# RWKV-6 attention and a tanh-shrink MLP on one core: empty TensorE instructions moved to the head of boot, and the first two weight loads put behind TensorE's work

## The chip, the cores and the metric

One Trainium2 chip, one NeuronCore of it. The time is device microseconds of one execution, from three runs of the kernel before: 545.66, 544.77 and 544.2, median 544.77 us. TensorE is called PE here (PEld is its weight load), VectorE DVE, ScalarE ACT, GpSimd POOL, SyncE SP. SP issues most of the DMAs.

## What is computed

```python
# r, k, v, w: (4, 8, 768, 48), u: (8, 48), f32
for t in range(S):
    cur = einsum('bhd,bhe->bhde', u * k_t, v_t)
    y_t = einsum('bhd,bhde->bhe', r_t, state + cur)
    state = w_t[..., None] * state + einsum('bhd,bhe->bhde', k_t, v_t)
x = y.transpose(0, 2, 1, 3).reshape(3072, 384)
h = x @ w_in            # 384 x 2048, weights of 64-bit width
g = h - tanh(h)
out = g @ w_out         # 2048 x 384
```

## The kernel before

The sequence of each batch is cut into two blocks of 384 tokens, eight blocks in all (`blocks`, line 1100). For one block the attention is computed in chunks of 64 tokens, for four pairs of heads, of which two at a time make a half (`HALVES`, `h1` the pairs 2 and 3, `h2` the pairs 0 and 1). The result `xT` (384 x 384, transposed) then runs through the MLP: for each of 16 tiles `f` of the hidden dimension, `first` (line 869) makes `h` with three products, `slight` (line 882) makes `g` from it on ACT and DVE, and `add` (lines 947 and 1001) multiplies `g` with `w_out`. The attention of the next block is spread among these tiles by a plan (line 1053) that says what runs at which `f`.

The order of all work on PE, SP, DVE and ACT is written out by hand: each engine runs its instructions in the order in which the Python code records them. An f32 product that is written once appears in the trace as two loads and two matmuls, so 24 written products of a group show as x48.

**Boot** (`boot`, line 1128) does the attention of block 0 before anything else. SP issues the inputs' loads and then the first raw weights. DVE scans the decays of half `h1` (`behind`, `before`), PE runs warm-up products on the identity (`passed`, `busy`; 94 of 16 columns, 11 of 512), and then, for `h1`: `own` (the products of k and r within a chunk), `turn_1` (six transposes), `earlier` (the products of k and r across the two decays), `update_half` (k by v), and later `from_scores` and `from_states`, which make the half's result in PSUM. In between and after come the same for `h2`. The masked copies of `own` and `earlier` into the scores are DVE's (line 502), `states_half` is a DVE scan (line 631), and `result_out` copies results into `late` and `xT` on ACT and DVE (line 729). In PE's order the second half runs `update_half(h2)`, `own(h2)`, one filler product, `earlier(h2)`, `from_states(h2)`, `from_scores(h2)`, and then the first tile of block 0 begins with `first` (line 871). The filler writes a PSUM tile of the first half's result, so it waits for ACT's copies of that result.

**The raw weights** come as 16 units of 768 KB (`load_weights`, line 248, in the order `UNITS`), each holding two tiles of `w_in` or `w_out` in 64-bit numbers. Five buffers hold them (`RAWS`). `convert` (line 253) makes f32 of one unit: three pieces on ACT (line 264) and one combination on DVE (line 268). `more_weights` issues the next unit's load on SP; `begin_behind(ins, then)` makes `then` wait for `ins`. Units 0 and 1 are `w_in` for the tiles 0 to 3, unit 2 is `w_out` for the tiles 0 and 1. The third load of boot waits for `own(h2)`, the fourth for `earlier(h2)`. In block 0 the pieces of conversion that ACT runs at tile `f` are counted in `PIECES`; ACT and DVE run in order, so a piece that moves changes what stands behind it.

**Empty instructions** on PE (`nop`, hint "apart") follow the products: `SPACED[i]` gives how many come after each product of `first` in block `i`, in the early and in the late tiles, and `add` puts one behind each of its own in most of block 0. PE's instructions are brought in by a DMA queue of their own, which the profile names "instruction".

The lines that the change touches are 76 and 80 (constants), `turn_1` (line 513) and `boot`.

Of the kernel before, what the change touches and what calls it, by code (L numbers as in the profile page):

```python
# [51 lines left out]
P = 128  # L52
# [20 lines left out]
RAWS = 5  # L73
LAG = 2
LAST = 5
PIECES = 0, 0, 2, 3, 3, 2, 4, 4, 3, 3, 3, 4, 4
UNITS = [(0, 0), (0, 1)] + [u for j in range(NF // 2 - 2) for u in ((1, j), (0, j + 2))] + [(1, NF // 2 - 2),
                                                                                      (1, NF // 2 - 1)]
LATE = 3
SPACED = (3, 0), (0, 3), (3, 2), (2, 3), (3, 2), (2, 3), (3, 0), (0, 0)  # L80

# [43 lines left out]
def kernel(  # L127
# [12 lines left out]
    nc = tc.nc  # L140
# [25 lines left out]
    ident = const.tile([P, P], F32, name="ident", tag="ident")  # L166
# [81 lines left out]
    def load_weights(n, queue):  # L248
        raw = conv.tile([P, 2 * DM, 2], I32, name="raw", tag="raw")
        src = weights[UNITS[n]].bitcast(I32).rearrange("p (n two) -> p n two", two=2)  # L250
        return *UNITS[n], raw, queue.dma_start(out=raw, in_=src)
# [46 lines left out]
    def scratch(ps):  # L298
        return ps.tile([P, 2, BANK], F32, name="att", tag="att")
# [14 lines left out]
    def begin_behind(ins, then):  # L314
        tc.add_manual_dep(then.ins, ins.ins.name, mybir.DependencyInfo(
            mybir.DependencyClass.Sync, mybir.DependencyReason.DATA))
# [3 lines left out]
    class Block:  # L320
# [186 lines left out]
        def own(self, ps, p0, **fill):  # L507
            return self.masked(ps, "k", "r", masks["diagonal"], p0, **fill)

        def earlier(self, ps, p0, **fill):  # L510
            return self.masked(ps, "post", "pre", masks["above"], p0, **fill)

        def turn_1(self, ps, p0):
            tp = scratch(ps)
            for p in range(UP):
                for c in range(NCP):
                    nc.tensor.transpose(tp[:, p, c * P:(c + 1) * P],
                                        self.chunk("post", p0 + p, 2 * c, n=2), ident)
            self.turned_as = tp

        def turn_2(self, p0):
# [347 lines left out]
    def first(xT, f, hp, apart=0):  # L869
        for kc in reversed(range(KC)):  # L870
            nc.tensor.matmul(hp, lhsT=w_in_sb[:, f, kc, :], rhs=xT[kc],  # L871
                             start=(kc == KC - 1), stop=(kc == 0))
            for _ in range(apart):
                nc.tensor.nop(nofuse=True, hint="apart")
        h = dense.tile([P, NB], F32, name="h", tag="h")
        return h, nc.scalar.activation(out=h, in_=hp, func=AF.Copy, scale=1.0 / UPSCALE)  # L876
# [228 lines left out]
    def more_weights(queue):  # L1105
        raws.append(load_weights(more_weights.n, queue))
        more_weights.n += 1
        return raws[-1][-1]
# [3 lines left out]
    def run(ops):  # L1112
        for op in ops:
            op()
# [13 lines left out]
    def boot(ps, pair, blk, later):  # L1128
        h1, h2 = HALVES
        blk.tiles["w"] = states0  # L1130
        for name, p0, n in (("w", h1 + 1, 1), ("w", h1, 1), ("k", h1, UP), ("r", h1, UP), ("w", h2, UP)):
            blk.load(name, p0, n)
        blk.load_v()
        blk.load("k", h2, UP)
        blk.load("r", h2, UP)
        more_weights(nc.sync)

        both = (h1, h1 + 1), (h2, h2 + 1)
        blk.behind(h1 + 1, 1)
        blk.behind(h1, 1)  # L1140
        blk.take_whole(h1, UP)
        blk.totals_by_column(h1)
        nc.scalar.copy(out=later_ident, in_=ident)
        blk.before(h1, UP)
        blk.times_behind(h1, UP)
        blk.times_u(h1, UP)
        own = blk.own(ps, h1, spare=94, ahead=5, late=6)
        blk.turn_1(ps, h1)
        blk.times_before(h1, UP)
        earlier = blk.earlier(ps, h1)  # L1150
        blk.behind(h2, UP)
        blk.take_whole(h2, UP)
        first_a, first_b = convert(*raws.pop(0), tiles=2)
        own()
        blk.turn_2(h1)
        blk.totals_by_column(h2)
        blk.update_half(pair, h1)
        begin_behind(blk.done, more_weights(nc.sync))
        blk.times_behind(h2, UP)
        blk.times_u(h2, UP)  # L1160
        blk.turn_1(ps, h2)
        blk.turn_2(h2)
        earlier()
        blk.results(ps)
        blk.result("from_scores", both[0])
        run(blk.states_half(h1))
        blk.result("from_states", both[0], True, apart=True)
        blk.before(h2, UP)
        blk.update_half(pair, h2)
        blk.times_before(h2, UP)  # L1170
        own = blk.own(ps, h2)
        own_scored = blk.done
        run(first_a[:1])
        blk.result_out((3,), [nc.scalar.copy] * 2)
        blk.result_out((2,))
        earlier = blk.earlier(ps, h2, ahead=1)
        scored = blk.done
        onwards = blk.states_half(h2)
        own()
        run(first_a[1:])  # L1180
        needed = 2 * KC - 2
        blk.fill_holes([nc.sync, nc.gpsimd], range(needed, 2 * KC))
        begin_behind(own_scored, more_weights(nc.sync))
        blk.fill_holes([nc.sync, nc.gpsimd], range(needed))
        begin_behind(scored, more_weights(nc.sync))
        later.load("w")
        second_a, second_b = convert(*raws.pop(0))
        third_a, third_b = convert(*raws.pop(0))
        run(second_a)
        more_weights(nc.sync)  # L1190
        blk.results(ps)
        blk.yp.reverse()
        blk.result("from_states", both[1], apart=True)
        earlier(1, 1)
        earlier(0, 1)
        for p in reversed(both[1]):
            blk.result("from_scores", (p,), True, more=True)
        later.load("k")
        more_weights(nc.sync)
        run(onwards)  # L1200
        run(first_b[:1])
        for p in reversed(both[1]):
            blk.result_out((p,), [nc.scalar.copy, nc.vector.tensor_copy])
        run(first_b[1:])
        run(third_a[:2])
        run(second_b)
        blk.held(0, NPAIR)
        return [(third_a[2], third_b)]
# [38 lines left out]
    for i, blk in enumerate(blocks):  # L1247
# [9 lines left out]
        for f in range(NF):  # L1257
# [4 lines left out]
            to = [acc[0], acc[1], hp, spare_a, spare_b, spare_a][now] if now < 6 else hp  # L1262
            h, made = first(here, f, to[:, 0:NB], SPACED[i][f > 12 + (i < 2)])
            if not i:
                made_up = converting(pieces, (PIECES[f] if f < len(PIECES) else 1) - 1)
                for op in ahead_of_h:
                    op()
                made_up += converting(pieces, 1 if f < len(PIECES) and PIECES[f] else 0)
            g, ahead_of_h, square, later_ops = slight(h, now, i, f)
# [184 lines left out]
```

## Time and profile before

| | |
|---|---|
| median of three runs | 544.77 us |
| the profiled execution | 545.84 us |
| its span, from first to last instruction | 544.1 us |
| granted PE clock, mean | 0.995 |
| PE, DVE, ACT busy | 533.7, 459.0, 403.8 us |
| DMA, mean of the span | 104 GB/s |

Times in the views are microseconds from the start of the span. A row of the timeline gives start, length, engine, line of the code, operation, tiles (out, then in), count, and in brackets the idle time of the engine before it with what ended it. Instructions of a kind that follow each other are merged into one row. A row of the stretches gives, for a window of time, how long each engine was busy (with its instructions), the clock that was granted to PE, and the DMA share and rate. A row of the waits gives who waited for whom, the total, how often, and the longest. PE's empty instructions are not in these views.

### The profile page before, as it was taken

What the parts mean: (1) busy time and instruction counts of PE and PEld (TensorE: products, weight loads), DVE (VectorE), ACT (ScalarE), POOL (GpSimd) and SP (SyncE); (2) the same over time, 40 slices, a digit from 0 to 9 for tenths busy, and PEclk for the clock granted to TensorE, in tenths of its full rate; (3) what the DMA queues carried; (4) which work ended last, traced back from release to release, by engine and by line L of the source; (5) the groups of instructions that cost most, each with busy time, mean ns of one, the idle gap of its engine ahead of it and who ended that gap; (6) DMA issues with size and microseconds to landing.
All of it is one profiled execution on the core that took longest, in us unless ns stands there. A gap on an engine that the chain in (4) does not pass through costs nothing.

```text
span 544.1 us, 14866 instructions
## 1 busy us (share of the span) xinstructions
PE 533.7 (98%) x5682; PEld 404.1 (74%) x5682; DVE 459.0 (84%) x943; ACT 403.8 (74%) x814; POOL 6.6 (1%) x47
## 2 busy tenths in 40 slices
PE   7899999999999999999999999999999999999996
PEld 5756666678887788777877787877878787787874
DVE  7889999999989989789897979879897997457564
ACT  5799996888668876688676886588866885666561
POOL 1100000000000000000000000000000000000000
PEclk9899999999999999999999999999999999999999
DMA  7798633251402631154212532137231420200101
GB/s 274 236 400 308 237 102 115 87 146 60 121 19 79 159 110 54 58 128 138 60 55 73 121 116 67 49 89 161 67 97 54 92 56 2 57 1 0 45 1 46
DMA packets 53048, 56.34 MB, mean 104 GB/s; under 512 B 21488, under 2 KB 50928, under 8 KB 52976
## 3 DMA queue, kind: packets, MB, share of 16 engines
q1 hardware_dynamic: 52592, 55.18, 33.8%
q8 instruction: 48, 0.79, 0.6%
q14 instruction: 24, 0.20, 0.1%
q10 hardware_dynamic: 288, 0.10, 0.1%
q0 software_dynamic: 96, 0.07, 0.1%
HBM read 44.73 MB, written 4.72 MB: 91 GB/s over the span
## 4 chain that ended last, share of the span: by engine, by line
PE 95%; DVE 2%; issue 1%; DMA 0%; PEld 0%; PEldq 0%; DVEq 0%; SPq 0%
PE hp L871 44%; PE acc L999 26%; PE att L999 7%; PE acc L950 5%; PE att L757 4%; PE att L494 2%; PE acc L977 2%; PE att L575 1%; PE att L871 1%; PE acc L871 1%; DVE post L429 1%; DVE scores L502 1%; DMA states<-in_wT 0%; DVE pre L417 0%; PE att L977 0%
## 5 line engine op out<-in xcount | busy, mean ns | idle before, releaser
L871 PE MATMUL hp<-xT,w_sb 128*128 128x384 f32 x738 | 259.2, 487 | 0.4 <-DVE w_sb L268 0.4
L871 PEld LDWEIGHTS hp<-xT,w_sb 128*128 128x128 f32 x738 | 131.9, 190 | 69.7 <-issue 0.5
L999 PE MATMUL acc<-forms,g 128*128 128x128 f32 x954 | 133.2, 276 | 0.0
L876 ACT ACTIVATE h<-hp 128x384 f32<-128x384 f32 x123 | 60.4, 491 | 97.3 <-PE hp L871 97.1
L999 PEld LDWEIGHTS acc<-forms,g 128*128 128x128 f32 x954 | 122.0, 192 | 10.3
L879 DVE SCALAR_TENSOR_TENSOR h<-h,s 128x384 f32<-128x384 f32 x128 | 70.5, 551 | 50.5 <-ACT s L894 50.4
L920 DVE TENSOR_TENSOR g<-g 128x256 f32<-128x256 f32 x265 | 103.1, 418 | 7.3 <-PE acc L999 6.5
L895 ACT ACTIVATE qa<-s,shift 128x384 f32<-128x384 f32 x113 | 69.5, 615 | 3.7
L897 ACT ACTIVATE junk<-s,shift 128x384 bf16<-128x384 f32 x113 | 67.7, 599 | 0.0
L879 DVE SCALAR_TENSOR_TENSOR g<-qa,h 128x384 f32<-128x384 f32 x112 | 61.6, 550 | 1.6 <-ACT qa L905 0.2
L894 ACT ACTIVATE s<-h 128x384 f32<-128x384 f32 x113 | 59.1, 523 | 3.5
L999 PEld LDWEIGHTS acc<-w_sb,g 128*128 128x128 f32 x318 | 46.8, 191 | 9.7 <-ACT sums L967 0.3
L999 PE MATMUL acc<-w_sb,g 128*128 128x128 f32 x318 | 53.1, 276 | 0.0
L999 PE MATMUL att<-w_sb,g 128*128 128x128 f32 x212 | 35.5, 275 | 0.0
L999 PEld LDWEIGHTS att<-w_sb,g 128*128 128x128 f32 x212 | 31.1, 192 | 5.3
L1034 DVE TENSOR_TENSOR sums<-sums 128x256 f32<-128x256 f32 x84 | 32.8, 406 | 1.7 <-ACT sums L1011 1.5
L950 PE MATMUL acc<-w_sb,sums 128*128 128x384 f32 x96 | 33.7, 487 | 0.0
L264 ACT ACTIVATE up<-raw 128x768 f16<-128x768 f32 (+1 forms) x32 | 33.1, 1069 | 0.0
L950 PEld LDWEIGHTS acc<-w_sb,sums 128*128 128x128 f32 x96 | 18.0, 190 | 12.3 <-DVE sums L879 0.3
L417 DVE TENSOR_TENSOR_SCAN pre<-w,start 128x780 f32<-128x780 f32 x14 | 25.0, 1783 | 0.8
L429 DVE TENSOR_TENSOR_SCAN post<-w,seed 128x780 f32<-128x780 f32 x14 | 24.8, 1774 | 0.0
L897 ACT ACTIVATION_READ_ACCUMULATOR junk<-s,shift 128x1 f32 x113 | 21.1, 187 | 0.0
(118 smaller groups left out, 529.2 us busy)
## 6 DMA issues: line engine op xcount, KB each, us to landing
raw<-in_weights SPq DMA_DIRECT2D x16, 768.0 KB, 5.9
w<-in_wT SPq DMA_DIRECT2D x7, 780.0 KB, 4.6
k<-in_kT SPq DMA_DIRECT2D x7, 768.0 KB, 4.6
r<-in_rT SPq DMA_DIRECT2D x7, 768.0 KB, 4.6
v_sb<-in_v SPq DMA_DIRECT2D x8, 576.0 KB, 3.9
k<-in_tokens SPq DMA_DIRECT2D x7, 576.0 KB, 5.2
r<-in_tokens SPq DMA_DIRECT2D x7, 576.0 KB, 4.7
out_y<-sums SPq DMA_DIRECT2D x18, 128.0 KB, 1.8
```

What stands on the lines that cost most here:

```text
L264: return lambda: nc.scalar.activation(out=to, in_=of, func=AF.Copy, scale=scale, bias=bias)
L429: return nc.vector.tensor_tensor_scan(out=back(t[:, 0:width]), data0=back(self.tile("w")[:, a:a + width]), data1=back(seed[:, 0:width]), i ...
L871: nc.tensor.matmul(hp, lhsT=w_in_sb[:, f, kc, :], rhs=xT[kc], start=(kc == KC - 1), stop=(kc == 0))
L876: return h, nc.scalar.activation(out=h, in_=hp, func=AF.Copy, scale=1.0 / UPSCALE)
L879: return lambda: nc.vector.scalar_tensor_tensor(out=out, in0=in0, scalar=scalar, in1=in1, op0=op0, op1=ALU.mult)
L894: nc.scalar.activation(out=s, in_=h, func=AF.Square)
L895: nc.scalar.activation(out=qa, in_=s, func=AF.Square, bias=shift[:, 4:5])
L897: nc.scalar.activation(out=junk[:, 0:NB], in_=s, func=AF.Relu, bias=shift[:, 5:6], accum_out=excess[:, at:at + 1])
L920: return lambda: nc.vector.tensor_tensor(out=G[:, to:to + 2], in0=two(G, g_at(q, a0), g_at(q, a1)), in1=two(G, g_at(q, b0), g_at(q, b1)), ...
L950: nc.tensor.matmul(acc, lhsT=g[:, j * P:(j + 1) * P], rhs=w_out_sb[:, f, :], start=(f == self.first), stop=(f == NF - 1))
L999: nc.tensor.matmul(to, lhsT=G[:, g_at(q, a), :], rhs=rhs, start=start, stop=stop, skip_group_check=True)
L1034: ops.append(lambda op=op, at=at: nc.vector.tensor_tensor(out=at[0], in0=at[1], in1=at[2], op=OPS[op]))
```

## The change

Four things. 80 empty instructions stand ahead of PE's first work in boot. In block 0 one empty instruction, not three, follows each product of `first` in the tiles 0 to 13, which is 84 fewer (14 tiles, 3 products, 2 each). The first raw load, which SP issued straight behind the inputs' loads, waits for `turn_1(h1)`; the second, which waited for `update_half(h1)`, waits for `from_scores(h1)`. And `PIECES` moves one piece of conversion from tile 6 to tile 5: on ACT one piece comes ahead of a `qa` and an `h`, and on DVE one combination comes ahead of one tile's `s`, `h`, `sums` and the second scan of `before`. All other instructions keep their order on their engines.

```diff
-PIECES = 0, 0, 2, 3, 3, 2, 4, 4, 3, 3, 3, 4, 4
+PIECES = 0, 0, 2, 3, 3, 3, 3, 4, 3, 3, 3, 4, 4
...
-SPACED = (3, 0), (0, 3), (3, 2), (2, 3), (3, 2), (2, 3), (3, 0), (0, 0)
+FRONT = 80
+SPACED = (1, 0), (0, 3), (3, 2), (2, 3), (3, 2), (2, 3), (3, 0), (0, 0)
...
         def turn_1(self, ps, p0):
...
-                    nc.tensor.transpose(tp[:, p, c * P:(c + 1) * P],
-                                        self.chunk("post", p0 + p, 2 * c, n=2), ident)
+                    self.done = nc.tensor.transpose(tp[:, p, c * P:(c + 1) * P],
+                                                    self.chunk("post", p0 + p, 2 * c, n=2), ident)
...
     def boot(ps, pair, blk, later):
...
         blk.load("r", h2, UP)
-        more_weights(nc.sync)
...
         blk.times_u(h1, UP)
+        for _ in range(FRONT):
+            nc.tensor.nop(nofuse=True, hint="apart")
         own = blk.own(ps, h1, spare=94, ahead=5, late=6)
         blk.turn_1(ps, h1)
+        begin_behind(blk.done, more_weights(nc.sync))
         blk.times_before(h1, UP)
...
         blk.update_half(pair, h1)
-        begin_behind(blk.done, more_weights(nc.sync))
...
         blk.result("from_scores", both[0])
+        begin_behind(blk.done, more_weights(nc.sync))
         run(blk.states_half(h1))
```

## The prediction

> **What bounds the kernel now.** First the page: busy time per engine, the instruction queue, and the chain that ended last; then who kept PE waiting.
>
> ```profile
> PE 533.7 (98%) x5682; PEld 404.1 (74%) x5682; DVE 459.0 (84%) x943; ACT 403.8 (74%) x814; POOL 6.6 (1%) x47
> ...
> q8 instruction: 48, 0.79, 0.6%
> ...
> PE 95%; DVE 2%; issue 1%; DMA 0%; PEld 0%; PEldq 0%; DVEq 0%; SPq 0%
> ...
> PE att L312 <- POOL ident masks.py:199: 2.1, 1, 2.1
> PE att L494 <- ACT k L454: 1.4, 1, 1.4
> PE att L494 <- issue: 1.2, 1, 1.2
> PE hp L871 <- DVE w_sb L268: 0.4, 1, 0.4
> ```
>
> PE sets the end, and the last rows are its idle time, longest first (two smaller ones are left out). All but the 0.4 fall before 25 us, in boot. So the change can win only in boot, by a faster PE clock, or not at all. The 1.2 that waits for "issue" (nothing the profile shows) comes in boot's second half. The timeline there, PE, DVE and ACT:
>
> ```profile
> 15.39 1.46 PEld L679 LDWEIGHTS att<-pre,first_states 48*48 48x48 f32 x38 [0.39 <-issue]
> ...
> 17.92 0.90 PE L494 MATMUL att<-r,k 48*64 48x64 f32 x48
> ...
> 19.07 0.68 PE L494 MATMUL att<-pre,post 48*64 48x64 f32 x29
> 19.42 0.73 DVE L631 TENSOR_TENSOR_SCAN first_states<-hp,first_totals 128x288 f32<-128x288 f32 x1
> ...
> 20.07 0.99 DVE L502 COPY_PREDICATED scores<-mask_all,att 128x768 f32<-128x768 uint8 x1
> ...
> 20.97 0.50 PE L494 MATMUL att<-pre,post 48*64 48x64 f32 x18 [1.22 <-issue]
> ...
> 21.62 1.07 DVE L502 COPY_PREDICATED scores<-mask_all,att 128x384 f32<-128x384 uint8 x2 [0.56 <-PE att L494]
> ...
> 23.49 1.53 PE L697 MATMUL att<-scores,v_sb 64*48 64x64 f32 x48 [0.24 <-DVE w_sb L268]
> ...
> 24.95 5.05 PE L871 MATMUL acc<-xT,w_sb 128*128 128x384 f32 x12
> ...
> 25.48 0.90 ACT L264 ACTIVATE w_sb<-raw 128x768 f32<-128x768 f32 x1
> 26.27 1.06 ACT L264 ACTIVATE up<-raw 128x768 f16<-128x768 f32 x1
> 28.11 0.49 ACT L876 ACTIVATE h<-acc 128x384 f32<-128x384 f32 x1 [0.78 <-PE acc L871]
> ```
>
> PE stops after 29 of the 48 products of `earlier(h2)`, in mid-stream with no wait in the program. DVE's copy of them waits 0.56 us. The granted clock, by stretches of 3.41 us:
>
> ```profile
> 0.00:19.75 19.75, 15.73 (x475) 11.78 (x475) 16.27 (x29) 12.25 (x19) 4.08 (x18) 1.00 0.70 237
> 13.18:16.59 3.41, 3.12 (x106) 2.73 (x99) 3.35 (x8) 2.66 (x5) 0.00 (x0) 1.00 0.63 210
> 20.01:23.42 3.41, 2.28 (x67) 2.14 (x67) 2.85 (x7) 2.53 (x3) 0.13 (x2) 1.00 0.87 269
> 23.42:26.84 3.41, 3.35 (x51) 2.52 (x52) 1.76 (x4) 2.21 (x4) 0.00 (x0) 0.50 0.96 350
> ```
>
> Columns: PE, PEld, DVE, ACT, POOL busy, then the clock, the DMA share, GB/s. The stretch with the stall has 67 small products; the next is granted half the clock. A stretch with 106 was not followed by that.
>
> The stall as a page boundary: until 19.75 us PE had issued 475 loads and 475 products; with 14 waits and drains in the listing that is 964 instructions. The queue named "instruction" brought 48 packets (0.79 MB, 16.5 KB each) for 11364 loads and products, 774 empties (listing) and some 60 waits: about 254 each, so I take pages of 256. Boundaries are then at 196, 452, 708, 964, 1220, and the stall stands on one. By the Trainium skill ("Runtime: NRT & Kernel Launch", Instruction fetch mechanics) instructions come in blocks of 256, the next fetched while the current one runs, the crossing "mostly hidden". The block size agrees; hidden it is not in this row. By that rule moving the boundaries is worth nothing, which is the second rival.
>
> How long a page takes, taking it that a crossing asks for the page after the one entered (then the third packet belongs to the stall): boundary 708 is the last load of `from_states(h1)`, at 16.85 (15.39 + 1.46); the packet of the page from 964 on runs inside 18.5 to 19.7 us; PE resumes at 20.97: **4.1 us** from crossing to resuming. For boundary 196 the crossing is in the warm-up products at 4.53 and the packet begins after 7.6, under loads that fill the DMA engines. The two windows of the DMA queues, after the row of the crossing:
>
> ```profile
> 4.53 2.14 PE L305 MATMUL att<-ident 128*128 128x512 bf16 x5
> ...
> q8 instruction: 1, 0.02, 5.3%
> ...
> q8 instruction: 1, 0.02, 5.4%
> ```
>
> So crossing to packet is 1.7 us when queues are quiet (18.5 - 16.85) and 3.1 when full: a page takes 4.1 to 5.5.
>
> **The change part by part.** *80 empties ahead.* No row prices one. Below: nothing. Above: a whole 16-column load and product.
>
> ```profile
> 2.08 2.51 PE L312 MATMUL att<-ident 128*16 128x16 bf16 x94 [2.08 <-POOL ident masks.py:199]
> ```
>
> 2.51/94 = 27 ns, so 80 cost 0 to 2.1 us. I take half a pair, 1.1 us, nearest to a bare instruction. They run while PE waits for `ident` until 2.08, and if they end later the warm-up moves into the 1.4 us for which PE waits for `times_u`: cost 0; without that cover 1.1. *84 fewer in block 0:* 0, as PE shows no idle time there but the 0.4; they are issued under products.
>
> *What 80 shifts.* Boundaries 452, 708, 964, 1220 now fall on what were 372, 628, 884, 1140: mid `earlier(h1)`, the start of `from_states(h1)` (15.39), product 38 of 48 of `own(h2)`, product 20 of 48 of `from_scores(h2)`. The page needed in `own(h2)` at 17.92 + 38/48 x 0.90 = 18.6 is asked for at 15.39 and comes at 15.39 + 4.1 = **19.5**: the stall shrinks from 1.22 to 0.9 and moves one product group ahead. There it has cover: DVE scans `first_states` until 20.15 (19.42 + 0.73) and reads `own(h2)` only then. `own` ends at 19.7, `earlier(h2)` some 1.3 later (0.68 + 0.50 and the filler product) at 21.0, and DVE copies it at 21.15 instead of 21.62: **0.4 to 0.5** won on the path to `from_scores(h2)`, 0.56 at most, as DVE's copy of `own` ends at 21.06. That group starts near 23.05; its page comes at 19.5 + 4.1 = 23.6, needed at 23.4: 0.2 lost. It ends at 23.6 + 28/48 x 0.9 = 24.1, not 25.02. In the page before, `from_states(h1)` is needed 3.7 us after mid `earlier(h1)` (11.23 + half of 0.93):
>
> ```profile
> 11.23 0.93 PE L494 MATMUL att<-pre,post 48*64 48x64 f32 x48
> ```
>
> so up to 0.4 of a stall, if PE's queue isn't ahead; I take 0, keep 0.4.
>
> *The clock.* From 20.01 to 23.42 PE now runs the rest of `own`, 48 of `earlier`, 48 of `from_states` and some of `from_scores`, over 106 products. I take the clock as full: half of 26.84 - 23.49, **1.7 us** of PE. The Trainium skill ("TensorE: Matmul & The Clock Gate", Part 1) tells of a free-running window of 3413 ns and half rate after an idle one; stretch and rate agree with the row, but 2.28 us of 3.41 busy is not an idle window.
>
> *The weights' loads.* When SP issued the first two, and how long the first, second and third took to land:
>
> ```profile
> 5.65 8.21 SPq L251 DMA_DIRECT2D raw<-in_weights  x2
> ...
> raw<-in_weights SPq DMA_DIRECT2D x1, 768.0 KB, 9.2
> ...
> raw<-in_weights SPq DMA_DIRECT2D x1, 768.0 KB, 4.5
> ...
> raw<-in_weights SPq DMA_DIRECT2D x1, 768.0 KB, 5.6
> ...
> 10.42 0.88 PE L517 MATMUL att<-ident,post 128*128 128x128 f32 x6
> 14.24 0.90 PE L697 MATMUL att<-scores,v_sb 64*48 64x64 f32 x48
> ...
> 14.98 0.90 ACT L264 ACTIVATE w_sb<-raw 128x768 f32<-128x768 f32 x1
> 16.54 0.97 ACT L729 COPY late<-att 48x384 f32<-48x384 f32 x2 [0.66 <-PE att L679]
> ...
> 18.87 1.05 SPq L251 DMA_DIRECT2D raw<-in_weights  x1
> ```
>
> The first was issued at 5.65 and took 9.2 behind the inputs (landed 14.85). Now SP waits with it for the turn (10.42 + 0.88 = 11.3; behind it stands only the second, which went at 13.5), it lands at 11.4 + 4.5 = 15.9, and ACT converts to 16.8: its 0.66 idle covers all but 0.3, which delays the `late` and `xT` copies alone (PE's filler product waits for them, at 19.7). No inputs are ahead of it now, so I bound it by 5.6: landed at 17.0, the copies done at 19.4, still in time. Early it can win nothing, as those copies wait for PE. The second goes at 15.2, lands by 19.7 (4.5) or 20.8 (5.6); ACT takes it at about 20. Queued behind it on SP are one row of `xT` and the **third** load, which also waits for `own(h2)`: 18.87 becomes 19.85, and with 5.6 it lands at 25.45. ACT converts it in two pieces (25.48 to 27.33 now, 1.85) and then copies `h` of the first tile: 25.45 + 1.85 = 27.3 against 28.11. So ACT, and DVE behind it, win only **0.8**, though PE, from 24.1, would be done with it near 26.2 (four such products take 1.45 in the row below).
>
> *Whose win counts.* Through block 0 DVE and ACT are nearly as full as PE (45.98 and 46.52 of 47.40 us):
>
> ```profile
> 30.00:77.40 47.40, 46.95 (x322) 28.64 (x321) 45.98 (x84) 46.52 (x68) 0.13 (x2) 1.00 0.76 273
> ...
> 76.66 0.54 DVE L879 SCALAR_TENSOR_TENSOR sums<-qa,h 128x384 f32<-128x384 f32 x1
> 77.38 1.45 PE L950 MATMUL acc<-w_sb,sums 128*128 128x384 f32 x4
> ```
>
> At 77.38 PE uses sums that DVE ended at 77.20: 0.2 to spare. PE's win beyond DVE's is lost there: 0.8 + 0.2 = **1.0 us**. *PIECES* takes one ACT piece and one DVE combine earlier; totals stay, the 0.4 wait of `hp` can go, but it is PE's alone: 0 in the sum, 0.4 at most.
>
> The sum: 544.1 - 1.0 = 543.1 of span; the profiled execution took 545.84, 1.74 outside the span and 1.07 above the median, so for the median 544.77 - 1.0 = **543.8 us**.
>
> **The rivals.** *All pages in time.* If a page comes within the 3.2 us from crossing to use, nothing stalls: `own` ends at 18.8, the third load lands at 24.5, `h` is copied at 26.35, 1.76 earlier; with 0.2 that is 1.96: **542.8**. For it: PE's queue may run ahead of what it executes and ask earlier. Against: 4.1 was measured that way too, and in a quiet DMA queue.
> *The shift does nothing.* The 1.22 is something else and stays with its products, or the clock drops all the same. Then at most the 0.4 is won, less what the later third load takes: 0.3, **544.5**.
> *Slower.* Pages queue behind the weights, now moved into the same 11 to 20 us, and take 5.5: `own(h2)` resumes at 20.9, its load lands at 26.85, `h` at 28.7, 0.6 late; `from_scores(h2)` gets its page at 26.4 and ends at 26.95, 1.9 late, and PE idles enough to halve the clock. DVE then loses about 1.2: **546.0**. It decides from 4.9 us a page (third load landing at 28.11 - 1.85 = 26.26).
>
> **How the numbers follow.** Forecast 0.42, pages in time 0.28, nothing moved 0.15, slower 0.15. Range 542.3 to 546.0: from 0.5 below the first rival (the 0.4 of `hp`, scatter) to the slower case; the forecast's own is 543.0 to 544.6 (loads of 4.5 to 5.6, a stall of 0 to 0.4 more). About 0.3%, 1.6 us, is what a measurement of this kernel can tell from no change, so below 543.1 is faster: most of the first rival and a tail of the forecast, 0.36. Above 546.4: the worse part of the last, 0.10. Between: 0.54.
>
> **What would show it.** The "issue" wait of `earlier(h2)` gone and one of some 0.9 us among the products of `own(h2)`; perhaps a short one in `from_scores(h2)`. Granted clock 1.00 from 23.42 to 26.84. The third load issued near 19.9 and `h<-acc` near 27.3. PE's lead some 1.9 us at 30 us and 1.0 at 78. It is wrong if the stall stays at the same product, if half the clock is granted in boot, if ACT waits for the first two loads, or if the leads at 30 and 78 us are equal.

## The result and the profile after

| | before | after |
|---|---|---|
| median | 544.51 us (4 runs, 544.2 to 545.66) | 551.7 us (4 runs, 551.6 to 552.69) |
| profiled execution | 545.84 us | 552.69 us |
| its span | 544.1 us | 551.0 us |
| mean granted clock | 0.995 | 0.993 |

The changed kernel takes 1.0132 times as long (95% interval 1.0113 to 1.0152): 7.2 us more, where 1.0 less was forecast. Who kept PE waiting (waiter, releaser, total, times, longest):

```profile
PE att L313 <- issue: 6.9, 1, 6.9
PE att L495 <- issue: 2.0, 1, 2.0
PE att L680 <- DVE start L417: 0.8, 1, 0.8
```

The code after has some of its lines one to three further down than before (L313 is L312 of before, L495 is L494). The wait for `ident` is now one for "issue", 6.9 us long. The chain that ended last shows that nothing else is ahead of it (start, length, what):

```profile
3.21 3.71 issue
6.93 2.50 PE att L313 x94
...
23.64 2.09 issue
31.18 5.83 PE acc L872 x12
```

The end now depends on PE from the first microseconds on. The timeline of boot:

```profile
6.93 2.50 PE L313 MATMUL att<-ident 128*16 128x16 bf16 x94 [6.93 <-issue]
...
11.47 2.77 PE L306 MATMUL att<-later_ident 128*128 128x512 bf16 x6
14.16 0.93 PE L495 MATMUL att<-r,k 48*64 48x64 f32 x48
...
15.24 1.03 DVE L503 COPY_PREDICATED scores<-mask_all,att 128x768 f32<-128x768 uint8 x1 [3.83 <-PE att L495]
...
20.51 1.56 PE L680 MATMUL att<-pre,first_states 48*48 48x64 f32 x37 [0.84 <-DVE start L417]
...
21.82 0.93 ACT L265 ACTIVATE w_sb<-raw 128x768 f32<-128x768 f32 x1 [2.15 <-DMA raw<-in_weights]
...
23.01 0.77 PE L495 MATMUL att<-r,k 48*64 48x64 f32 x38
25.73 0.44 PE L495 MATMUL att<-r,k 48*64 48x64 f32 x10 [1.96 <-issue]
26.21 0.33 SPq L252 DMA_DIRECT2D raw<-in_weights  x1
```

The same group of before, in its timeline:

```profile
9.41 0.79 PE L494 MATMUL att<-r,k 48*64 48x64 f32 x28 [1.39 <-ACT k L454]
```

PE's first product comes at 6.93 instead of 2.08, and the products of `own(h1)` at 14.16 instead of 9.41 (4.75 later), where DVE now waits 3.83 for them. The third load goes at 26.21, not 18.87. The stall among small products is 1.96 long, after 38 of the 48 of `own(h2)`. And the stretches of 3.41 us around it (PE, PEld, DVE, ACT, POOL busy, clock, DMA share, GB/s):

```profile
21.06:24.47 3.41, 2.60 (x119) 2.34 (x116) 2.99 (x4) 2.60 (x5) 1.05 (x2) 1.00 0.58 217
24.47:27.88 3.41, 2.15 (x78) 1.85 (x78) 1.68 (x3) 3.41 (x5) 0.66 (x4) 1.00 0.32 66
27.88:31.30 3.42, 3.18 (x85) 2.85 (x84) 1.60 (x6) 1.28 (x3) 0.00 (x0) 0.50 0.94 331
31.30:34.71 3.41, 3.41 (x6) 1.89 (x7) 2.44 (x5) 2.19 (x3) 0.00 (x0) 0.50 1.04 388
```

Two stretches at half clock behind the stall, where the profiled execution of before had one. So from one profiled execution to the other PE is 4.75 us later at `own(h1)`, 6.2 at the first tile (31.11 in its timeline against 24.95) and 6.9 at the end (the spans).

### The profile page after: what moved, and what is told of

Read it like the earlier page. It is cut to its first block, busy times and chain, and to the rows that moved or that the text cites. A ratio compares the mean times of both kernels' runs of the same rounds, so it can differ in the third digit from the quotient of the medians.

```text
span 551.0 us, 14863 instructions
## 1 busy us (share of the span) xinstructions
PE 536.1 (97%) x5682; PEld 405.1 (74%) x5682; DVE 459.5 (83%) x943; ACT 403.8 (73%) x814; POOL 6.6 (1%) x47
## 4 chain that ended last, share of the span: by engine, by line
PE 94%; issue 2%; PEld 1%; DVE 1%; POOL 0%; PEldq 0%; ACT 0%; POOLq 0%
PE hp L872 43%; PE acc L1000 26%; PE att L1000 6%; PE acc L951 5%; PE att L758 4%; PE att L495 2%; PE acc L978 2%; PE att L576 2%; PE acc L872 1%; PE att L872 1%; PE att L306 1%; PEld att L680 0%; PE att L313 0%; PE att L518 0%; PEld att L495 0%
## 5 line engine op out<-in xcount | busy, mean ns | idle before, releaser
L503 DVE COPY_PREDICATED scores<-mask_all,att 128x768 f32<-128x768 uint8 (+1 forms) x19 | 17.8, 969 | 5.6 <-PE att L495 5.6
```

## The experiments

Theory: the empty instructions have a price of their own that their cover doesn't hold (the first 4.75 us), and the later loads cost the rest. Rivals: the shifted pages cost it, or PIECES, or the 84 fewer in block 0. Each kernel was timed beside the kernel before, whose median was 544.4 to 544.8 us in every group of runs. Diffs are against the kernel before, where nothing else is said.

### Loads and PIECES without the empties

```diff
-PIECES = 0, 0, 2, 3, 3, 2, 4, 4, 3, 3, 3, 4, 4
+PIECES = 0, 0, 2, 3, 3, 3, 3, 4, 3, 3, 3, 4, 4
...
-        more_weights(nc.sync)
...
         blk.turn_1(ps, h1)
+        begin_behind(blk.done, more_weights(nc.sync))
...
-        begin_behind(blk.done, more_weights(nc.sync))
...
         blk.result("from_scores", both[0])
+        begin_behind(blk.done, more_weights(nc.sync))
```

As in the change, `turn_1` hands on its last transpose here and wherever a load waits for `turn_1(h1)`; the diffs below don't show that line again.

> The kernel before with only the later weight loads and the moved piece; the empties stand as before (none ahead, three behind each product of the first tiles). If the empties cost the 7 us: 544.0 to 545.3 us, PE's first product at 2.1, own(h1) at 9.4, the 1.2 us stall still in earlier(h2), half a clock behind it. If the later loads cost a part: 546 to 549, with ACT waiting for the first load ahead of the copies of the first result.

Measured: 546.95 us (12 runs, 545.02 to 548.14), ratio 1.0039 (1.0026 to 1.0052), 2.3 us more than before. Its timeline, then its stretches:

```profile
15.61 0.92 ACT L265 ACTIVATE w_sb<-raw 128x768 f32<-128x768 f32 x1 [0.25 <-DMA raw<-in_weights]
...
22.07 0.50 PE L495 MATMUL att<-pre,post 48*64 48x64 f32 x18 [1.81 <-issue]
```

```profile
20.78:24.20 3.42, 2.13 (x67) 2.13 (x67) 2.04 (x6) 2.29 (x3) 0.13 (x2) 1.00 0.80 244
24.20:27.62 3.42, 3.18 (x55) 2.32 (x52) 1.77 (x4) 1.90 (x4) 0.00 (x0) 0.50 0.93 347
```

ACT waits only 0.25 us for the first raw load, as forecast (0.3). But the stall in `earlier(h2)` has grown from 1.22 to 1.81 us, and half a clock follows.

### Empties without the loads

```diff
+FRONT = 80
+SPACED = (1, 0), (0, 3), (3, 2), (2, 3), (3, 2), (2, 3), (3, 0), (0, 0)
...
+        for _ in range(FRONT):
+            nc.tensor.nop(nofuse=True, hint="apart")
         own = blk.own(ps, h1, spare=94, ahead=5, late=6)
```

> The kernel before with only the empties: 80 ahead, 84 fewer in block 0; loads and pieces as before. If the empties cost the 7 us: 550.5 to 552 us, PE's first product at 6.9, own(h1) at 14.2. If the later loads cost a part of it: 547 to 549.5.

Measured: 549.67 us (4 runs, 548.49 to 550.58), ratio 1.0079 (1.0056 to 1.0103), 5.1 us more: below the first case (550.5 to 552), just above the second. Its timeline:

```profile
6.93 2.50 PE L313 MATMUL att<-ident 128*16 128x16 bf16 x94 [6.93 <-issue]
...
13.04 0.57 PE L495 MATMUL att<-r,k 48*64 48x64 f32 x23
```

The first product is 4.85 us late and `own(h1)` 3.63: here the 1.4 us of idle time ahead of it did cover part. The two halves of the change, 5.1 and 2.3, add up to 7.4, against the 7.2 of the whole.

### The same shift by products, with the later loads

Against the changed kernel: no empties ahead, and 40 more warm-up products of 16 columns (80 instructions) in their place:

```diff
-FRONT = 80
+FRONT = 0
...
-        own = blk.own(ps, h1, spare=94, ahead=5, late=6)
+        own = blk.own(ps, h1, spare=134, ahead=5, late=6)
```

> The changed kernel with 40 more 16-column warm-up products (80 instructions, 27 ns a product, 1.1 us) in place of the 80 empties: the same shift of all that follows, without their time. If only the empties' price was wrong and the rest of the forecast holds: own(h1) at 9.4, the stall in own(h2) at 0.9 to 1.1 us, full clock from 23.4 us, 543.0 to 544.3 us. If the page in own(h2) comes as late as in the changed kernel (2.0 us) and the clock halves again: 544.5 to 546.5.

Measured: 548.65 us (6 runs, 547.64 to 550.18), ratio 1.0072 (1.0053 to 1.0092), above both cases of the expectation. In its timeline ACT waits 1.88 us for the first raw load, and the stall in `own(h2)` is the longest of all kernels:

```profile
17.73 0.91 ACT L265 ACTIVATE w_sb<-raw 128x768 f32<-128x768 f32 x1 [1.88 <-DMA raw<-in_weights]
...
22.09 0.44 PE L495 MATMUL att<-r,k 48*64 48x64 f32 x10 [2.50 <-issue]
```

Without the price of the empties the change still costs 4.0 us; against the change itself, the empties cost 3.1 (551.7 - 548.65). `own(h1)` starts at 10.32 here, not 9.4, as the six last wide products take 2.77 us, as in after.

### The same shift by products, loads as before

```diff
-SPACED = (3, 0), (0, 3), (3, 2), (2, 3), (3, 2), (2, 3), (3, 0), (0, 0)
+SPACED = (1, 0), (0, 3), (3, 2), (2, 3), (3, 2), (2, 3), (3, 0), (0, 0)
...
-        own = blk.own(ps, h1, spare=94, ahead=5, late=6)
+        own = blk.own(ps, h1, spare=134, ahead=5, late=6)
```

> The kernel before with the 40 extra warm-up products and the 84 fewer empties, but with the weight loads and pieces where they were. If the loads' place doesn't matter to the pages: as the run with both, within 0.5 us. If the first load's packets hold up the page that is asked for in earlier(h1): a stall at the first product of from_states(h1), 0.5 to 1.5 us slower than that run.

Measured: 545.48 us (12 runs, 544.43 to 546.6), ratio 1.0015 (1.0003 to 1.0027). It is 3.2 us faster than with the later loads, which neither case of the expectation had, and 4.2 faster than with 80 empties in the products' place (549.67). The profiled execution, at 544.43 us the fastest of the twelve, did what the forecast had hoped for: a stall of only 0.31 in `own(h2)` and full clock in boot.

```profile
19.62 0.44 PE L494 MATMUL att<-r,k 48*64 48x64 f32 x10 [0.31 <-issue]
...
24.07 0.91 PE L871 MATMUL acc<-xT,w_sb 128*128 128x384 f32 x2
```

The first tile starts at 24.07, not 24.95, and yet the kernel is 0.9 us slower in the median. So the shift, done by products in the empties' place, isn't worth what the forecast gave it; what the 0.9 is, with no timed run at a low clock, is open.

### PIECES alone

```diff
-PIECES = 0, 0, 2, 3, 3, 2, 4, 4, 3, 3, 3, 4, 4
+PIECES = 0, 0, 2, 3, 3, 3, 3, 4, 3, 3, 3, 4, 4
```

> The kernel before with the change of PIECES alone. The later weight loads with PIECES made the kernel 2.3 us slower in the median, and PIECES took the 0.4 us wait of PE for w_sb away there without the end moving. Theory (PIECES is worth nothing at the end): within 0.3 us of before, PE some 0.4 ahead between 55 and 77 us and level again from 80 us; the row hp <- DVE w_sb is gone. Rival (PIECES, which moves an ACT piece ahead of an h, is what costs the 2.3): 546 to 547 us.

Measured: 544.5 us (12 runs, 543.64 to 547.45), ratio 1.0004 (0.9987 to 1.002). Its waits of PE; those left out are 0.3 us or less, and none is of `hp`:

```profile
PE att L312 <- POOL ident masks.py:199: 2.1, 1, 2.1
PE att L494 <- issue: 1.5, 1, 1.5
...
PE acc L950 <- DVE sums L879: 0.2, 1, 0.2
```

The 0.4 that `hp` waited for `w_sb` is gone, and 0.2 that `acc` waits for DVE's `sums` at 78.4 us has come: PIECES is worth nothing that these runs can tell. The runs also show what goes with a low clock: eight with a mean clock of 0.998 or more took 543.6 to 545.0 us, three with 0.992 or 0.993 took 547.3 to 547.5. One of the three is the profiled one, whose 3 us hold a stall of 1.49 and two stretches at half clock; the other two have no trace.

### Each later load alone

The first load behind `turn_1(h1)`, the second left behind `update_half(h1)`:

```diff
-        more_weights(nc.sync)
...
         blk.turn_1(ps, h1)
+        begin_behind(blk.done, more_weights(nc.sync))
```

> The kernel before with the first raw load behind turn_1(h1) and the second left behind update_half(h1). Theory (the second load is what hurts, because its traffic falls on the packet of the page that is asked for in from_states(h1)): the stall in earlier(h2) stays near 1.2 to 1.5 us, ACT waits under 0.5 us for the first load, and the time is within 0.7 us of before. Rival (the first load is what hurts, because without a load started under the inputs all conversion is later): ACT waits some 1.5 to 2 us for the first raw load, PE waits for late or xT, and the time is 546.5 us or more.

The second behind `from_scores(h1)`, the first left at the head:

```diff
-        begin_behind(blk.done, more_weights(nc.sync))
...
         blk.result("from_scores", both[0])
+        begin_behind(blk.done, more_weights(nc.sync))
```

> The kernel before with the second raw load behind from_scores(h1) and the first left at the head. Theory (the second load holds up the page): from the crossing at the end of from_states(h1) to the packet of the next page pass 2.3 us or more instead of 1.7, the stall in earlier(h2) is 1.7 to 2.2 us, and the time is 1 to 2 us above before. Rival (the page does not care which load runs): the stall stays at 1.2 us and the time is within 0.5 us of before.

Measured: 548.05 us (5 runs, 545.81 to 548.77), ratio 1.0065 (1.0052 to 1.0078), and 547.87 us (5 runs, 547.33 to 548.19), ratio 1.0058 (1.0045 to 1.0071). The first theory, that the first load alone does no harm, is wrong. The second is right about the stall (1.7 to 2.2 expected) and too low for the time. Each load alone costs more than both with PIECES. The stall is 1.81 with the first and 2.07 with the second; the trace of the first is of its fastest run, 545.81 us, while the other four took 547.1 us or more. In the second kernel, the timeline and the stretches:

```profile
22.04 0.50 PE L494 MATMUL att<-pre,post 48*64 48x64 f32 x18 [2.07 <-issue]
```

```profile
19.63:23.04 3.41, 1.34 (x57) 1.20 (x51) 1.97 (x4) 3.27 (x4) 0.13 (x2) 1.00 0.83 255
23.04:26.45 3.41, 3.17 (x86) 2.84 (x83) 1.60 (x6) 0.50 (x2) 0.00 (x0) 0.50 0.85 243
```

### 40 empties, and 12

```diff
+FRONT = 40
...
+        for _ in range(FRONT):
+            nc.tensor.nop(nofuse=True, hint="apart")
```

> The kernel before with 40 empty instructions ahead of PE's first work and nothing else changed. Theory (each empty has a price of 61 to 72 ns that nothing covers beyond the wait for ident): the first warm-up product comes at 1.2 + 40 x 0.07 = 4.0 us, which is 2.0 later than before and, with the 80 of the changed kernel at 6.9, gives a slope of 72 ns; own(h1) is 0.5 to 1.5 us later and the time 0.5 to 2 us above before. Rival (the 4.85 us is a fixed cost, a page that the empties make late): the first product comes at 2.1, or at 6.9 as with 80.

> The kernel before with 12 empty instructions ahead of PE's first work and nothing else changed. Theory (72 ns each, from 1.1 us on): they end at 1.1 + 12 x 0.072 = 2.0 us, inside the wait for ident, so the first warm-up product stays at 2.08 us, own(h1) starts at 9.4 and the time is within 0.7 us of before. Rival (any empties ahead cost a fixed start, or shift the page boundaries to a worse place at once): the first product comes after 2.5, or the time is 1.5 us or more above before.

Measured with 40: 548.51 us (4 runs, 548.03 to 549.99), ratio 1.0083 (1.0069 to 1.0098). With 12: 544.73 us (10 runs, 544.15 to 545.32), ratio 0.999 (0.9973 to 1.0007). The timelines, 40 and then 12:

```profile
4.01 2.50 PE L313 MATMUL att<-ident 128*16 128x16 bf16 x94 [4.01 <-POOL mask_all L201]
...
10.31 0.93 PE L495 MATMUL att<-r,k 48*64 48x64 f32 x48
...
25.54 0.33 PE L698 MATMUL att<-scores,v_sb 64*48 64x64 f32 x8 [1.56 <-issue]
```

```profile
2.08 2.51 PE L313 MATMUL att<-ident 128*16 128x16 bf16 x94 [2.08 <-POOL ident masks.py:199]
...
6.63 1.60 PE L306 MATMUL att<-later_ident 128*128 128x512 bf16 x6
...
9.38 1.08 PE L495 MATMUL att<-r,k 48*64 48x64 f32 x48 [1.15 <-ACT k L455]
```

From 40 to 80 empties the first product goes from 4.01 to 6.93: **73 ns each**, so the first is issued near 1.1 us, and 12 of them (to 2.0) hide under the wait for `ident`. The price is settled, as both traces with 80 start at 6.93. The time of the 40, twice the most that was expected, is not: `own(h1)` is only 0.9 late, and the other 3 us of the 4.1 come behind it, with a stall of 1.56 in `from_scores(h2)`, to which the page boundary has moved, and a stretch at half clock.

### The kernel before once more

> The kernel before once more, unchanged, for the trace of another of its executions. Of 40 timed runs of it 35 lie between 543.7 and 545.3 us with a mean clock of 0.997 to 1.000, and two at 547 with 0.993. Theory (the profiled execution of before, 545.84 us at 0.995, was dearer than the kernel's usual run because of the half clock at 23.4 to 26.8 us, so that the 1.7 us that the forecast meant to win there were in the median already): at a mean clock of 0.998 or more the time is 544.0 to 544.8 us, no stretch between 20 and 34 us is at half clock, the first tile takes less than 5 us for its 12 products, and the stall in earlier(h2) is there all the same at 1.0 to 1.5 us. Rival (the half clock belongs to the stall and is in every run): a stretch between 20 and 34 us is at 0.50 here too, or the stall is gone with it.

Measured: 545.5 us at a mean clock of 0.999, one run. Its timeline and stretches:

```profile
9.33 1.08 PE L494 MATMUL att<-r,k 48*64 48x64 f32 x48 [0.98 <-ACT k L454]
...
16.25 1.57 PE L679 MATMUL att<-pre,first_states 48*48 48x64 f32 x38 [0.28 <-PEq L717]
...
19.90 0.97 PE L494 MATMUL att<-pre,post 48*64 48x64 f32 x48
```

```profile
20.01:23.42 3.41, 3.07 (x96) 2.81 (x97) 3.28 (x8) 3.38 (x4) 0.13 (x2) 1.00 0.86 237
23.42:26.84 3.42, 2.63 (x53) 1.71 (x54) 2.66 (x5) 2.59 (x4) 0.00 (x0) 1.00 0.89 309
```

No stall and no half clock: `earlier(h2)` runs its 48 products through. The stall was expected to stay, and the time to be under 544.8. So the two rows on which the forecast's gain rested are not in every execution: of the four traces whose boot is that of before (this one, before, PIECES alone, 84 fewer alone) three have both. One run settles nothing about the time, as runs of before in this group with a mean clock above 0.995 lie between 543.7 and 546.3. For the kernel as a whole the mean clock is known for 80 timed runs: 72 lie above 0.995.

The page also comes otherwise than the prediction took it. `from_states(h1)`, whose last load was to ask for it, starts 0.8 later than in before (16.25 against 15.43) and ends its loads at 17.7, but the packet of the queue "instruction" begins at 17.91, 0.6 earlier than in before (18.54): 0.2 us behind that crossing, not 1.7. What asks for a page is thus not this crossing alone, and stays open.

### 84 fewer in block 0, alone

```diff
-SPACED = (3, 0), (0, 3), (3, 2), (2, 3), (3, 2), (2, 3), (3, 0), (0, 0)
+SPACED = (1, 0), (0, 3), (3, 2), (2, 3), (3, 2), (2, 3), (3, 0), (0, 0)
```

> The kernel before with one empty instruction instead of three behind each product of the first MLP step in block 0, and nothing else. Theory (they are issued under products and cost nothing, so 84 fewer win nothing): within 0.4 us of before, PE's lead over the kernel before the same at 30 and at 80 us but for the clock. Rival (an empty instruction costs its 72 ns there too): 84 x 0.072 = 6 us of PE won by 75 us, of which what DVE and ACT allow reaches the end, 543 us or less; or PE and DVE meet badly and it is 1 us slower.

Measured: 547.13 us (12 runs, 546.2 to 550.72), ratio 1.005 (1.0031 to 1.0069), slower by 2.4, more than the 1 us of the rival's second case. Its waits of PE, the two longest behind `ident`:

```profile
PE att L757 <- issue: 1.8, 4, 0.7
PE att L494 <- issue: 1.8, 1, 1.8
```

Line 757 is the small products of the attention in the later blocks, and neither the kernel before nor the one after has such a wait there. Each of the four ends 1.3 to 1.6 us behind the end of a packet of the queue "instruction", so they are waits for pages: 84 fewer shift every boundary from block 0 on, and four now fall among small products. With 80 more instructions at the head (empties or products) the shift is 4, and no trace has such waits. So the two edits of the empties belong together.

### The shift at no cost in time

44 more warm-up products of 16 columns, 4 fewer of 512, which is 80 more instructions:

```diff
-SPACED = (3, 0), (0, 3), (3, 2), (2, 3), (3, 2), (2, 3), (3, 0), (0, 0)
+SPACED = (1, 0), (0, 3), (3, 2), (2, 3), (3, 2), (2, 3), (3, 0), (0, 0)
...
-        own = blk.own(ps, h1, spare=94, ahead=5, late=6)
+        own = blk.own(ps, h1, spare=138, ahead=3, late=4)
```

> The kernel before with 44 more warm-up products of 16 columns and 4 fewer of 512 columns (at half clock 44 x 27 ns = 1.2 us for 4 x 0.43 = 1.7 us), and one empty instruction instead of three in block 0; loads and PIECES as before. This shifts the pages by 80 instructions, as the change does, at no cost in time. Theory (the shift itself takes the stall out of earlier(h2), but the third load and DVE keep the first tile where it was): own(h1) at 9.4 us or before, a stall under 0.6 us in own(h2), 543.5 to 544.8 us. Rival (the shift is worth what the forecast said): 543.3 us or less; or (the shift is bad whatever pays for it): 545.5 us or more.

Measured: 545.44 us (12 runs, 544.58 to 547.9), ratio 1.0016 (1.0001 to 1.0031). Its timeline:

```profile
9.33 1.08 PE L494 MATMUL att<-r,k 48*64 48x64 f32 x48 [0.82 <-ACT k L454]
...
19.54 0.44 PE L494 MATMUL att<-r,k 48*64 48x64 f32 x10 [0.58 <-issue]
```

`own(h1)` is on time, the stall 0.58 (0.9 forecast) and in the place forecast, and the kernel is 0.7 us slower, not faster: just under the 545.5 of the second rival. The shift on its own wins nothing.

### The second load earlier

The later loads cost 2.3 us or more; was it their packets in the air while a page is asked for? Then the loads moved the other way should help. Both at the head, and the second behind `turn_1(h1)`:

```diff
         more_weights(nc.sync)
+        more_weights(nc.sync)
...
-        begin_behind(blk.done, more_weights(nc.sync))
```

> The kernel before with the second raw load issued straight behind the first, at the head, instead of behind update_half(h1): the opposite of what the change does. Theory (a raw load in the air when the page for earlier(h2) is asked for delays it, the stall grows past 1.2 us and PE's clock is halved behind it): with both loads landed by 16 us the page comes in time, the stall is 0 to 0.6 us, no stretch between 20 and 34 us is at half clock, at most 1 timed run in 8 has a mean clock of 0.995 or less, and the time is 543.5 to 544.7 us. Rival (when the second load runs does not matter, and the later loads cost because the weights come later): the stall and the half clock appear as in the profiled execution of before, in some runs more than in 1 of 8, and the time is 544.5 us or more; or the second load takes the inputs' bandwidth, own(h1) starts after 9.8 us and the time is 545 us or more.

```diff
         blk.turn_1(ps, h1)
+        begin_behind(blk.done, more_weights(nc.sync))
...
-        begin_behind(blk.done, more_weights(nc.sync))
```

> The kernel before with the second raw load behind turn_1(h1), issued near 11.4 us instead of 13.5. Theory (as for both loads at the head, without the inputs' bandwidth in the way): landed near 16 us, ahead of the page that is asked for at 16.9; stall 0 to 0.6 us, no half clock between 20 and 34 us, at most 1 timed run in 8 at a mean clock of 0.995 or less, 543.5 to 544.6 us. Rival (the second load's time does not matter): stall near 1.2 us in the trace or half clock in more than 1 run in 8, 544.5 us or more.

Measured: 546.52 us (6 runs, 545.36 to 547.96), ratio 1.0037 (1.0024 to 1.0051), and 548.14 us (5 runs, 546.84 to 548.59), ratio 1.0058 (1.0044 to 1.0071). The theory as it stood falls: the stall is 1.53 and 1.81, not under 0.6. The DMA queues say more. From 12.4 to 14.6 us, the kernel before (packets, MB, share of 16 engines), and then the second of these two:

```profile
q1 hardware_dynamic: 68, 0.31, 41.8%
q8 instruction: 1, 0.02, 3.8%
```

```profile
q1 hardware_dynamic: 168, 0.89, 100.0%
```

In this stretch before brings a page; with a load in the way none comes (nor with both at the head, queue 1 at 99.1%, nor with the first load behind `turn_1(h1)`, at 93.3%). From 16.9 to 19.0 us, the kernel before, and the one with the second load alone behind `from_scores(h1)`:

```profile
q1 hardware_dynamic: 25, 0.07, 8.8%
...
q8 instruction: 1, 0.02, 3.1%
```

```profile
q1 hardware_dynamic: 120, 0.71, 83.2%
```

Here it is the next page that comes later. By this reading there are two stretches in boot in which a page is fetched, and the second load of before (issued at 13.5; queue 1 is at 80.1% from 14.6 to 16.9) runs between them; moved either way, it meets one. The packets of queue 8 tell how far this reading holds (us):

```
                               first page  second page      PE
kernel                         begins      begins   ends    resumes
before                         13.96       18.54    19.57   20.97
before once more               13.83       17.91    18.94   no stall
PIECES alone                   13.89       18.45    19.93   21.16
84 fewer alone                 13.89       19.17    20.13   21.46
second load later              13.94       19.38    20.56   22.04
second load at the head        14.74       19.07    20.19   21.61
both later and PIECES          14.81       19.48    20.63   22.07
first load later               14.95       19.24    20.81   22.13
second load sooner             15.37       19.68    21.16   22.57
shift by products              12.99       17.26    18.24   19.62
both later, shift by products  14.00       19.77    20.73   22.09
80 empties, 84 fewer           15.76       20.84    21.98   23.25
after                          16.83       23.50    24.46   25.73
```

In all twelve traces with a stall PE resumes 1.2 to 1.5 us behind the end of the second page's packet: the stall is the wait for that page. For the first page the reading holds in every group with the same instructions ahead of it: a load moved into its stretch makes it begin 0.8 to 1.5 us later. Where only the first page met a load (second load at the head, first load later, second load sooner) the second begins 4.3 us behind it, against 4.1 to 5.3 in the first four rows, so the delay is passed on to the stall. That a load also holds up the second page directly isn't shown: with 84 fewer alone, whose boot and loads are those of before, the packet begins at 19.17 with queue 1 at 7.3% in the stretch, as late as with some of the moved loads (19.07 to 19.68).

### All together

The stall is the longest "issue" wait of PE behind the head, in the profiled execution; the stretches at half clock are those between 20 and 36 us in it; the last column counts timed runs whose mean clock was 0.995 or less.

```
                                 stall   half-clock  timed runs
kernel                           us      stretches   <= 0.995
before                           1.22    1           8 of 80
before once more                 none    0
PIECES alone                     1.49    2           4 of 12
12 empties                       0.35    0           0 of 10
40 empties                       1.56    1           1 of 4
80 empties, 84 fewer             1.16    2           1 of 4
84 fewer alone                   1.8     2           3 of 12
shift by products                0.31    0           0 of 12
shift at no cost                 0.58    0           1 of 12
first load later                 1.81    0           4 of 5
second load later                2.07    2           5 of 5
both later and PIECES            1.81    1           11 of 12
both later, shift by products    2.50    1           5 of 6
second load at the head          1.53    0           3 of 6
second load sooner               1.81    1           5 of 5
after                            1.96    2           4 of 4
```

With the loads where before has them, 18 of 146 runs have the low clock; with a load moved, 37 of 43. The 146 leave out the single run of before once more. No trace without a stall of 1.1 us or more has a half-clock stretch there, and of the twelve with such a stall ten have one.

## Why the prediction was wrong

**80 empties ahead: 0 to 2.1 us, 1.1 taken, all covered.** This step failed. Against products that shift as much, the 80 cost 3.1 of the change's 7.2 us (551.7 against 548.65), and with the loads of before 4.2 of 5.1 (549.67 against 545.48). A whole 16-column load and product (27 ns) was taken as the upper bound of an empty, as if less work had to mean less time. Measured is 73 ns, so that 80 take 5.8 us. The covers named were right: the wait for `ident` holds 12, and the 1.4 us ahead of `own(h1)` was used with 80 empties alone (4.85 late at the first product, 3.63 at `own(h1)`). In the profiled execution of after even that was gone, and `own(h1)` was 4.75 late: the six last wide products took 0.46 us each (2.77 / 6) instead of 0.28 (1.65 / 6 with 80 empties alone). These 1.1 us are not the price of the empties, as the kernel with products and later loads shows them too.

**Where the boundaries fall.** Right to the product: `own(h2)` is cut after 38 of 48 in after, and in the kernels that shift by products its last 10 stand behind the stall. Ahead of `from_states(h1)`, where "up to 0.4" was named and 0 taken, PE waited 0.84 in after. The row puts it down to DVE's `start`, which ended at 20.11, 0.4 before PE went on at 20.51; the first page's packet ended at 19.05, 1.46 before, as ahead of the stalls in the table of packets. That it was the page fits, and isn't shown.

**A page takes 4.1 us from crossing to resuming.** Failed as a property of the kernel. In before once more, products that stand behind the same boundary were not held up at all, and the packet began 0.2 us behind the crossing, not 1.7; with the second load later the stall was 0.85 longer. What holds is smaller: PE resumes 1.2 to 1.5 us behind the packet's end, and DMA traffic in the first page's stretch goes with a packet that begins 0.8 to 1.5 us later.

**The clock, 1.7 us, and the 1.0 us won.** Failed in its base. Half a clock was read off one execution, and the win subtracted from a median that hardly has it: 72 of 80 timed runs of before ran above 0.995. The two traces of before differ in it: one has a half-clock stretch from 23.42, the other none. By the Trainium skill ("TensorE: Matmul & The Clock Gate", Part 1) the clock's window is free-running, so that the slow start of the same kernel differs from run to run. The two traces agree: their record of the full clock starts at 6.36 us in one and at 7.15 in the other. The shift without the price of the empties came to 545.4 to 545.5 us in two kernels, 0.7 and 0.9 more than before, and neither won anything.

**The first two loads, 0.3 us of delay and hidden.** This step failed too. For the first load's own arrival it was right without the empties (ACT waited 0.25); in after the load took until 21.82 and ACT waited 2.15. For the cost it was wrong: the two cost 2.3 us with PIECES, which alone cost nothing. The mechanism was in the text, as the slower rival (pages queue behind the weights, PE idles, the clock halves) at 0.15 and 546.0 us; without the empties the measurement is 546.95. It was priced 1 us too low and thought unlikely because 1.7 us from crossing to packet was taken for the quiet case that would apply. How much of the 2.3 is the late pages and how much the clock behind them, the runs don't separate.

**84 fewer in block 0: 0.** Right within the change, for a reason that the text missed: only the 80 at the head keep the later blocks' boundaries where they were. Alone it costs 2.4.

**PIECES: 0.** Right: no change in time, and PE waits 0.2 for DVE's sums near 78 us where it had gained 0.4.

**The rival in which no page is late,** 542.8, fell with the base: the traces nearest to it, before once more (no stall), 12 empties (0.35) and the shift by products (0.31), took 545.5, 544.67 and 544.43. **The rival in which the shift does nothing,** 544.5, was right that the shift wins nothing, though the shift alone came out 0.9 to 1.0 above it. By the rule of the Trainium skill that the prediction put beside it ("Runtime: NRT & Kernel Launch", Instruction fetch mechanics: a crossing is mostly hidden) moving boundaries wins nothing. That it wins nothing agrees, the reason doesn't: the table shows stalls of 0.3 to 2.5 us in every trace but one.

**Left open:** what asks for a page, and what sets the wait for it when the queues are quiet (1.22 to 1.8 us of stall in three traces whose boot is that of before, none in a fourth); the 0.7 to 0.9 us of the shift alone; why each later load alone costs more than both with PIECES (3.4 to 3.6 against 2.3 us); and most of the 4.1 us that 40 empties cost.

## What to carry to other kernels

Price an instruction that does nothing by running some of them, not by the shortest one that does something; ahead of the first work all that the first wait doesn't cover stands on the path. Before a win is built on a stall or a clock drop, look whether it is in a second execution, and compare the profiled time with the median that the win is taken from. A bulk load that runs while a page of instructions is fetched went with a later page here, so a load has good and bad places, and an edit that adds or removes instructions early moves the page boundaries all through the kernel.

## What the hardware showed beyond that

An empty TensorE instruction took 73 ns where nothing covered it, more than twice a 16-column load and product of the warm-up (27 ns). PE resumed 1.2 to 1.5 us behind the end of a page's packet. And of the 3.41 us stretches by which the clock is granted, those with 1.34, 2.13 and 2.15 us of small products were followed by one at half clock, though PE was busy for more than a third of each. Busy time alone doesn't tell: 2.28 in before was followed by half a clock, 2.11 with the first load later (18.21 to 21.62) and 2.21 with the second load at the head (17.87 to 21.28) were not.
